# A newly drawn issue order for an attention stage, with eight of its steps on other engines

## The chip, the cores and the metric

One core of one Trainium2 chip runs one program: a gated linear attention followed by two mixture-of-experts layers. The metric is device microseconds of one execution.

## The reference, cut to what matters

```
mag = sqrt(a_re^2 + a_im^2);  scale = min(mag, 0.999) / (mag + 1e-6);  a = (a_re + i*a_im) * scale
for t in range(768):                       # for each of 4 batches x 8 heads, head size 48
    S = a[t][:, None] * S  +  k[t][:, None] * v[t][None, :]      # complex state 48 x 48
    y[t] = q[t] @ real(S)
x = y as 3072 tokens x 384
x = moe(x)        # top-1 of 8 experts, 384 -> 1024 -> 384, relu
out = moe2(x)     # the same form, with a bias by modality in the gate
```

## The kernel before, in words

The recurrence is computed in chunks of 128 tokens. Within a chunk the product of the decays is an exponential of a running sum of logarithms, so a chunk becomes a few matmuls. There are 24 chunks (4 batches x 6); two neighbours of one batch form a unit, so there are 12 units, n = 0 to 11, three to a batch. A unit's elementwise tiles are 128 x 768 (two chunks of 128 x 384, which is 8 heads x 48).

A unit is a list of named steps, each a Python function that issues one to sixteen instructions:

- `ldar ldai ldq ldk ldv` load the five inputs (SyncE's DMA queue).
- `ck` clamps a_re, `sq1` squares it (`x1`), `sq3` squares a_im (`x3`), `ad` adds the two; `ln2 ex2` and `tt` make a_im/a_re, `at` its arctangent; `ln1 ex3 su` make the logarithm of the clamped magnitude.
- `lh ll` split that logarithm into an upper fp16 cast and the rest; `th tl` do the same with the angle. `pL pT` (one per chunk, hence `pL0 pL1`) take the running sums of both with triangular matmuls. `R Ri` are the exponentials of plus and minus the sum, `fi f` take whole turns off the angle, `ab sn cs` make sine and cosine. `cf` and `re` hand the angle and the decay of the unit's last token to the next unit.
- `qR kR` scale q and k. Eight products per unit, `hq/hk` with `c` or `s` (times cosine or sine) and the chunk number, fill the buffers `qhb` and `khb`: `hqs0` is q times sine of chunk 0, `hkc1` is k times cosine of chunk 1.
- For each half chunk (0 to 3): `Tq Tk` transpose on TensorE, `eq ek` copy the result out of PSUM to `qT kT`, `sc` makes the scores, `A` masks them out of PSUM, `py` applies them to v and to the state, `pu` makes the state's update. Per chunk: `S` adds the update to the state, `xe` copies y out of PSUM, `pt` turns it back (and makes the gate's logits), `ye` copies that to `yt`, `lg` sums the logits, `st_` stores. `Sr` decays the state between two units of one batch.

Every engine works its queue off in the order in which the steps are issued. That order isn't worked out in the kernel: each step of unit n has a number in the table `AT` (units 0, 1, 10 and 11 have tables of their own in `AT_OF`), all steps are sorted by n plus that number, and issued in this order. So one step's place in the order says behind which others it stands on its engine. Steps whose names begin with `z` belong to the setting up and to the first expert layer's early work; they keep their numbers. `ENG` says on which engine a step runs that has a choice: A is ScalarE, V is VectorE, P is GpSimd; a copy that isn't in it runs on ScalarE, a product on VectorE. Each step's PSUM bank exists once (`pq pk sc py pu pt pL pT`), so a bank's next matmul waits for the copy that empties it.

The two expert layers behind attention are limited by TensorE and aren't touched.

Of the kernel before, what the change touches and what calls it, by code (L numbers as in the profile page):

```python
# [19 lines left out]
P = 128  # L20
# [19 lines left out]
    zq3=-275.454, ldarb=-273.404, zq2=-255.701, ckb=-206.468, ldara=-199.491, sq1b=-184.693, ln2b=-177.867, zq4=-176.094, cka=-173.23, ldaia=-168.532,  # L40
    sq1a=-158.557, ex2b=-157.908, ln2a=-148.937, sq3a=-139.255, ldaib=-128.596, ldka=-126.962, ada=-126.443, ex2a=-123.863, zq0=-121.356,
    tta=-120.389, ttb=-118.361, zi=-114.402, ln1a=-111.569, zq1=-108.288, sq3b=-107.648, ex3a=-104.749, adb=-93.3771, ata=-91.9742,
    sua=-87.6725, lha=-86.8068, tha=-85.6312, atb=-85.4597, ln1b=-75.4824, tla=-71.2593, ldkb=-69.7035, zw0=-67.7862, ldqa=-67.0486, ex3b=-62.1188,
    thb=-60.4308, lla=-60.1911, zw1=-59.0382, sub=-58.6209, tlb=-57.2903, aba=-54.563, zk0=-53.3853, ldva=-52.7552, sna=-51.9432,
    zw2=-50.8688, lhb=-50.689, qRa=-50.6436, csa=-50.0341, kRa=-49.9225, llb=-49.2676, zw3=-47.5465, ldqb=-42.6622, kRb=-42.4287, zld=-36.0444,
    abb=-34.9246, qRb=-34.251, zw4=-33.8895, csb=-32.1312, snb=-29.7056, zk1=-28.5196, ldvb=-24.0754, zk3=-22.0775, zk2=-20.375, zwh7=-20.0527,
    zwh5=-7.0878, zwh6=-6.1043, ldar=-4.0093, ldai=-3.5899, zf=-3.5878, ck=-3.439, sq3=-3.3275, sq1=-3.1932, ln2=-2.968, ad=-2.8853, ln1=-2.4349,
# [4 lines left out]
    sc0=-0.218, Tq1=-0.2076, ek1=-0.1952, eq1=-0.1787, Tk2=-0.1725, A0=-0.1374, pu0=-0.1229, pu1=-0.0981, Tq2=-0.0816, sc1=0.0506, eq2=0.0589,
    py0=0.0692, A1=0.0795, ek2=0.0816, Tk3=0.0837, Tq3=0.1064, sc2=0.1498, zj=0.1705, A2=0.2304, eq3=0.2386, py1=0.2428, ek3=0.2676, sc3=0.3192,
    S0=0.3254, A3=0.3419, xe0=0.375, pu2=0.4948, py2=0.5072, py3=0.5155, pu3=0.5857, S1=0.7469, pt0=0.8006, Sr=0.9845, xe1=0.999, ye0=1.0899,
    lg0=1.1043, pt1=1.1767, lg1=1.5816, ye1=1.6167, dn0=1.7428, st_0=1.8915, st_1=2.2262, zwl6=2.6952, dn1=2.9886, zwh0=9.4349, zx=18.5444,
# [4 lines left out]
    zl1=146.621, zv3=157.976, zn1=162.009, zn2=187.836, zb1=246.1, zn3=246.175, zy=248.185, zp0=248.274, zp1=248.392, zp2=248.534, zp3=248.627, zp4=248.734,)  # L60
# [3 lines left out]
        pT0=-67.7841, fi0=-67.0196, f0=-61.7138, pL0=-59.0403, R0=-54.7304, Ri0=-52.6787, pT1=-50.8709, fi1=-48.9452, hqs0=-48.6126, pL1=-47.5486,  # L64
        hkc0=-46.3151, Ri1=-45.7758, f1=-44.5775, hqc0=-44.189, cf=-43.3068, hks0=-42.0072, R1=-41.8275, Tq0=-40.999, Tk0=-40.2118, eq0=-39.78,
        ek0=-34.7779, re=-33.8915, Tq1=-33.8833, pu0=-33.0424, eq1=-31.7944, Tk1=-31.2138, sc0=-28.9019, ek1=-27.7924, hks1=-27.3977, hkc1=-24.9845,
        Tk2=-24.9783, A0=-24.6705, ek2=-22.8791, hqs1=-22.187, pu1=-19.2097, sc1=-18.5548, py0=-18.3192, hqc1=-18.0548, A1=-16.0692, Tq2=-15.5424,
# [3 lines left out]
    1: dict(
        ldar=-101.743, ldai=-94.0919, zf=-94.0899, ck=-78.2841, sq1=-71.2758, ln2=-62.5919, sq3=-59.3006, ad=-55.8564, ex2=-50.3502, ln1=-47.8006,
        tt=-44.28, ex3=-43.3419, ldq=-42.2159, at=-41.03, su=-38.5258, lh=-38.2614, th=-34.9928, tl=-34.2366, pT0=-32.1126, ll=-29.8523,
        fi0=-28.1663, pL0=-27.2324, f0=-25.7634, R0=-25.1539, Ri0=-24.9597, pT1=-24.4494, fi1=-24.249, f1=-23.437, pL1=-22.5754, Ri1=-19.7717,
        cf=-18.9824, ab=-17.8481, R1=-17.1808, qR=-16.1147, sn=-15.53, cs=-14.5795, hqs0=-14.4411, ldk=-13.3378, kR=-12.6105, hkc0=-12.47,
        hqc0=-11.9556, hks0=-10.6271, hkc1=-6.2696, Tq0=-6.0733, eq0=-5.8998, Tk0=-5.7469, hks1=-4.2407, ek0=-4.1023, Tk1=-3.5527, sc0=-2.6519,
        hqs1=-1.9267, ek1=-1.7986, Tk2=-1.6539, Tq1=-1.3874, A0=-1.3585, ldv=-1.2862, re=-1.0837, eq1=-1.063, sc1=-1.0134, ek2=-0.939, A1=-0.9329,
        py0=-0.8977, Tk3=-0.844, hqc1=-0.7965, py1=-0.7448, ek3=-0.6767, pu0=-0.6229, Tq2=-0.5093, xe0=-0.4163, eq2=-0.3254, sc2=-0.2386, Tq3=-0.1498,
        eq3=0.0114, A2=0.0134, S0=0.1126, pt0=0.1643, sc3=0.1952, A3=0.2118, pu2=0.2324, py2=0.2469, py3=0.3399,),
    10: dict(  # L80
        Ri0=-1.4969, ab=-0.9638, Tk0=-0.032, ek0=0.249, eq0=0.5548, Tk1=0.7965, pu0=1.3833, Tq1=1.7056, eq1=1.7221, sc0=1.8233, A0=1.9039, Tq2=2.5052,
        pu1=4.282, ek1=4.3357, sc1=6.6333, eq2=8.0424, A1=8.8523, Tk2=10.8171, ek2=11.3936, py0=11.5196, py1=11.8605, xe0=12.7758, Tq3=13.1808,
        sc2=14.2779, Tk3=14.4721, eq3=14.5258, ek3=15.125, pt0=15.8254, ye0=16.5362, S0=16.5795, A2=17.3647, sc3=18.7283, pu2=20.2593, pu3=21.189,
        A3=21.687, lg0=24.0486, st_0=24.3998, py2=24.78, py3=25.3316, S1=28.3151, Sr=28.7014, xe1=30.6519, pt1=32.5238, ye1=35.8667, st_1=37.718,
        lg1=39.4762,),
    11: dict(
        sq3=-3.125, fi0=-1.5816, Ri0=-1.4225, pT1=-0.97, fi1=-0.5837, f1=-0.4329, pL1=-0.3027, ab=0.5919, R1=0.6353, qR=5.7779, Ri1=6.187, sn=6.5754,
        kR=7.5733, cs=8.0961, hkc0=9.6684, hqs0=12.8295, hqs1=14.9143, hqc0=15.2924, Tq0=15.4494, hks0=15.656, Tk0=15.9411, ek0=16.0465, eq0=16.6374,
        hqc1=16.9535, Tk1=22.094, ek1=22.8709, hkc1=23.1684, hks1=23.2614, Tq1=23.4143, sc0=24.344, A0=25.4597, Tk2=26.6705, eq1=29.7717, sc1=31.0878,
        Tq2=31.3853, A1=31.9494, ek2=32.1395, Tk3=32.4928, ek3=32.5899, pu0=32.7076, py0=33.0527, eq2=33.1787, py1=36.0196, sc2=36.4618, A2=39.3626,  # L90
        Tq3=39.4329, pu1=40.0651, xe0=41.1663, S0=41.3977, pt0=44.0857, eq3=44.9432, sc3=45.3048, A3=45.5878, ye0=45.8481, py2=45.8729, py3=46.7035,
        lg0=49.6787, xe1=52.1539, st_0=55.6457, pt1=58.3812, lg1=61.6312, ye1=62.8647, dn0=66.0238, st_1=67.1457, dn1=72.3027, dn2=79.4783,),
# [1232 lines left out]
```

## Time and profile before

| | |
|---|---|
| time, median of 3 runs | 803.96 us (799.52 to 807.28) |
| the profiled execution | 801.56 us, of which its span 799.8 us |
| attention's steps, by the trace | 0 to about 283 us of the span |
| the rest | the two expert layers |

Read it like this: the profiled execution's time is its span plus 1.8 us around it, and all rows below are of that execution. A stretch is given in microseconds from the span's start. "Busy" is the time in which an engine's instructions ran, waits inside an instruction included.

### The profile page before, as it was taken

To read this page: it belongs to the slowest core of one execution; us is meant where nothing else is said; L and a number is where in the kernel's file an instruction comes from. 1 tells how busy PE (TensorE), PEld (TensorE's weight loads), DVE (VectorE), ACT (ScalarE), POOL (GpSimd) and SP (SyncE) were. 2 spreads that over 40 slices of the span, in tenths; PEclk is the share of its full clock that TensorE was granted. 3 is DMA by queue.
4 is the path that set the end of the run, shared out by engine and by line. 5 is a ranking of instruction groups with operands and counts; after the bars stand their busy time and mean duration, and the time that the engine had idled before them with its cause. 6 is when DMAs were issued, how large, how long until landed. Compare 5 with 4: busy or idle time off the path is not lost. (4 is left out here: it accounts for less than half of the span.)

```text
span 799.8 us, 23480 instructions
## 1 busy us (share of the span) xinstructions
PE 736.1 (92%) x8451; PEld 595.8 (74%) x8451; DVE 562.9 (70%) x1437; ACT 469.2 (59%) x1008; POOL 284.2 (36%) x266
## 2 busy tenths in 40 slices
PE   7787889989898998999999999999898999999995
PEld 3475769768786976878787877788676787877873
DVE  8889999999999877575747486864473345545455
ACT  7797788787796525473737465675322345533453
POOL 5556575565676121221221224221121221312211
PEclk9898999998999999999999999999998999999998
DMA  9949674775433151625334252524033111511110
GB/s 185 249 80 197 143 150 120 169 153 122 93 81 100 38 202 34 208 56 185 110 126 161 87 191 76 187 70 169 19 99 133 41 58 46 208 52 42 60 44 29
DMA packets 159262, 91.41 MB, mean 114 GB/s; under 512 B 131804, under 2 KB 149764, under 8 KB 159104
## 3 DMA queue, kind: packets, MB, share of 16 engines
q1 hardware_dynamic: 151872, 68.49, 33.3%
q0 software_dynamic: 7232, 21.05, 8.5%
q8 instruction: 71, 1.16, 0.6%
q14 instruction: 87, 0.71, 0.3%
HBM read 192.54 MB, written 20.84 MB: 267 GB/s over the span
## 5 line engine op out<-in xcount | busy, mean ns | idle before, releaser
L817 PEld LDWEIGHTS <-wh 128*128 128x128 f16 x1296 | 127.9, 99 | 14.3 <-ACTq L882 6.4
L818 PEld LDWEIGHTS <-wh 128*128 128x128 f16 x1296 | 127.7, 99 | 7.9 <-issue 1.0
L819 PEld LDWEIGHTS <-wl 128*128 128x128 f16 x1296 | 127.8, 99 | 0.0
L838 POOL DMA_INDIRECT x<-yo,r1ids x27 | 31.8, 1178 | 182.2 <-ACT yo L837 126.0
L741 DVE SCALAR_TENSOR_TENSOR wl<-ws,wh 128x768 f16<-128x768 f32 x88 | 82.8, 952 | 15.4 <-ACT wh L740 7.5
L740 ACT ACTIVATE wh<-ws 128x768 f16<-128x768 f32 x88 | 74.1, 845 | 10.3 <-ACTq L852 4.8
L830 PE MATMUL mpu<-wh,hl 128*128 128x384 f16 x216 | 70.5, 327 | 5.2 <-DVE hl L822 4.4
L830 PEld LDWEIGHTS <-hl 128*128 128x128 f16 x432 | 42.4, 98 | 43.8 <-DVE hl L822 13.0
L830 PE MATMUL mpy<-wh,hl 128*128 128x384 f16 x216 | 71.1, 329 | 3.1 <-DVE hl L822 1.8
L828 PE MATMUL mpy<-wh,hh 128*128 128x384 f16 x216 | 71.2, 330 | 0.8 <-ACT hh L821 0.8
L817 PE MATMUL msc<-xh,wh 128*128 128x128 f16 x384 | 68.0, 220 | 3.8 <-ACTq L882 3.8
L829 PE MATMUL mpy<-wl,hh 128*128 128x384 f16 x216 | 71.0, 329 | 0.0
L828 PE MATMUL mpu<-wh,hh 128*128 128x384 f16 x216 | 70.4, 326 | 0.0
L829 PE MATMUL mpu<-wl,hh 128*128 128x384 f16 x216 | 70.4, 326 | 0.0
L817 PE MATMUL mpk<-xh,wh 128*128 128x128 f16 x384 | 68.0, 220 | 1.8 <-ACTq L882 1.8
L838 POOL DMA_INDIRECT out_dram<-yo,r2ids x21 | 21.1, 1005 | 134.8 <-ACT yo L837 127.6
L819 PE MATMUL mpq<-xh,wl 128*128 128x128 f16 x384 | 68.4, 220 | 0.0
L817 PE MATMUL mpq<-xh,wh 128*128 128x128 f16 x384 | 68.4, 220 | 0.0
L818 PE MATMUL mpq<-xl,wh 128*128 128x128 f16 x384 | 68.4, 220 | 0.0
L819 PE MATMUL msc<-xh,wl 128*128 128x128 f16 x384 | 68.1, 220 | 0.0
L818 PE MATMUL msc<-xl,wh 128*128 128x128 f16 x384 | 68.1, 220 | 0.0
L819 PE MATMUL mpk<-xh,wl 128*128 128x128 f16 x384 | 68.1, 220 | 0.0
(510 smaller groups left out, 2270.9 us busy)
## 6 DMA issues: line engine op xcount, KB each, us to landing
ws<-in_moe_w_dram SPq DMA_DIRECT2D x100, 1536.0 KB
ar<-in_a_re_dram SPq DMA_DIRECT2D x24, 192.0 KB
ai<-in_a_im_dram SPq DMA_DIRECT2D x24, 192.0 KB
k<-in_k_dram SPq DMA_DIRECT2D x24, 192.0 KB
q<-in_q_dram SPq DMA_DIRECT2D x24, 192.0 KB
v<-in_v_dram SPq DMA_DIRECT2D x24, 192.0 KB
x<-zero SPq DMA_DIRECT2D x8, 576.0 KB
x<-yt SPq DMA_DIRECT2D x24, 192.0 KB
```

The lines of the kernel that those rows point to most:

```text
L740: nc.scalar.activation(H_,S_,AF.Copy,scale=WS,accum_out=s.fl[:,s.n:s.n+1]); s.n+=1
L741: if lo: nc.vector.scalar_tensor_tensor(L_,S_,WS,H_,op0=ALU.mult,op1=ALU.subtract)
L817: nc.tensor.matmul(o,W.h1[:,d,fs],x.h[:,d,:],start=(d==0),stop=False)
L818: nc.tensor.matmul(o,W.h1[:,d,fs],x.l[:,d,:],start=False,stop=False)
L819: nc.tensor.matmul(o,W.l1[:,d,fs],x.h[:,d,:],start=False,stop=(d==ND-1))
L828: nc.tensor.matmul(o,hh[:,r,:],W.h2[:,f,:],start=(f==0),stop=False)
L829: nc.tensor.matmul(o,hh[:,r,:],W.l2[:,f,:],start=False,stop=False)
L830: nc.tensor.matmul(o,hl[:,r,:],W.h2[:,f,:],start=False,stop=(f==NF-1))
L838: nc.gpsimd.indirect_dma_start(out=s.dst,out_offset=bass.IndirectOffsetOnAxis(ap=R.ids[:,j:j+1] if ids is None else ids(),axis=0),in_=y,in ...
```

## The change: what it does

All numbers of `AT` and `AT_OF` for attention's own steps are new; the `z` steps keep theirs. Eight kinds of step change engine in units 1 to 11: `sq1`, `lh` and `eq2` go from VectorE to ScalarE, `ek0`, `ek1` and `ye0` from ScalarE to VectorE, `hqs0` and `hkc1` from VectorE to GpSimd. Unit 0 has the same for its copies and products, but of its half-wide passes only `sq1a` (to ScalarE) and `tta` (from GpSimd to VectorE) move. Two steps get the code for it:

```
 AT=dict(
...
-    ex2=-2.1973, ex3=-2.1849, su=-2.0713, lh=-2.061, tt=-1.9721, at=-1.8171, th=-1.8089, tl=-1.7655, ll=-1.7159, pL0=-1.6663, pT0=-1.6333,
...
+    ex3=-2.5125, ex2=-2.4717, su=-2.4082, tt=-2.3592, lh=-2.0144, at=-1.9704, ll=-1.6353, pL0=-1.6327, th=-1.6191, ldq=-1.6042, tl=-1.5858,
...
 ENG=dict(
-    ek0="A", ek1="A", ek2="A", ek3="A", eq0="A", eq1="A", eq3="A", xe0="A", xe1="A", ye0="A", ye1="A", Sr="P", hkc0="P", hks0="P", hks1="P", hqc1="P",
-    hqs1="P", kR="P", kRa="P", kRb="P", qR="P", sq3="A", tt="P", tta="P", ttb="P", eq2="V", hkc1="V", hqc0="V", hqs0="V",
-    qRa="V", qRb="V", sq1="V", sq1a="V", sq1b="V", sq3a="V", sq3b="V", th="V", tha="V", thb="V",)
+    ek2="A", ek3="A", eq0="A", eq1="A", eq2="A", eq3="A", lh="A", sq1="A", sq1a="A", sq3="A", xe0="A", xe1="A", ye1="A", Sr="P", hkc0="P", hkc1="P",
+    hks0="P", hks1="P", hqc1="P", hqs0="P", hqs1="P", kR="P", kRa="P", kRb="P", qR="P", tt="P", ttb="P", ek0="V", ek1="V", hqc0="V", lha="V", lhb="V",
+    qRa="V", qRb="V", sq1b="V", sq3a="V", sq3b="V", th="V", tha="V", thb="V", tta="V", ye0="V",)
...
-        def sq1(nm,s,sl): eng(nm).tensor_mul(s(tile_("x1")),s(u.x2),s(u.x2))
+        def sq1(nm,s,sl):
+            if ENG[nm]=="A": nc.scalar.activation(s(tile_("x1")),s(u.x2),AF.Square)
+            else: eng(nm).tensor_mul(s(tile_("x1")),s(u.x2),s(u.x2))
...
-        def lh(nm,s,sl): V.tensor_scalar(out=s(tile_("lh",F16)),in0=s(u.x1),scalar1=CS,scalar2=None,op0=ALU.mult)
+        def lh(nm,s,sl):
+            t=s(tile_("lh",F16))
+            if ENG.get(nm,"V")=="A": nc.scalar.activation(t,s(u.x1),AF.Copy,scale=CS)
+            else: V.tensor_scalar(out=t,in0=s(u.x1),scalar1=CS,scalar2=None,op0=ALU.mult)
```

Sorted by these numbers, one unit's worth of the middle of the stage reads as follows (n is the unit whose scores are made; a plus counts units ahead, a minus units behind; GpSimd's list begins where its queue turns to the scaling of q):

```
before
VectorE  A0(n) f1(+1) su lh(+2) eq2(n) A1(n) lg0(-1) ad(+3) cf(+1) th(+2) A2(n) tl ll(+2) re(+1) S0(n) A3(n) hqs0 hqc0(+1) ck(+4) lg1(-1) fi0 f0(+2) hkc1(+1) S1(n) sq1(+4) fi1(+2)
ScalarE  ln2(+3) ek2(n) ye0(-1) at(+2) eq3(n) ab(+1) ek3(n) sn(+1) xe0(n) cs(+1) Ri0 R0(+2) ln1(+3) ye1(-1) sq3(+4) ek0 eq0(+1) ex2(+3) ek1(+1) ex3(+3) eq1(+1) Ri1 R1(+2) xe1(n)
GpSimd   qR kR hks0 hkc0 hqs1 hks1 hqc1(+1) Sr(n) tt(+3)
after
VectorE  A0(n) re(+1) lg1(-1) cf(+1) A1(n) ll th(+2) ad(+3) S0(n) tl(+2) A2(n) ye0 lg0(n) fi0(+2) hqc0(+1) A3(n) f0(+2) ek0(+1) ck(+4) su(+3) fi1(+2) S1(n) f1(+2) ek1(+1)
ScalarE  at(+2) eq2(n) sq3(+3) ab(+1) ek2(n) sn(+1) ye1(-1) xe0 eq3(n) cs(+1) ek3(n) R0 Ri0(+2) ln1 ln2 ex3(+3) eq0(+1) ex2(+3) R1(+2) xe1(n) Ri1(+2) eq1(+1) sq1(+4) lh(+3)
GpSimd   qR kR hks0 hqs0 hkc0 hks1 hqs1 hkc1 hqc1(+1) tt(+3) Sr(n)
```

On the load queue, at the start, the first half of unit 0's v and unit 1's q, which stood ahead of the first expert's weights (two loads of 1,536 KB), stand behind them, and unit 1's a_re stands ahead of the second half of unit 0's a_im. Later on, the load queue keeps the same loads and stores in another order; the loads that matter for a unit still stand half a unit and more ahead of its first use. On TensorE, unit 1's `pT0 pL0 pL1 pT1` stand ahead of unit 0's `Tq1`, where they stood behind its `Tk1`.

## Rows read from the trace of the kernel before

**Rows 1.** The page: span in 40 equal slices, busy tenths; PEclk is the granted clock.
```profile
PE   7787889989898998999999999999898999999995
...
DVE  8889999999999877575747486864473345545455
...
PEclk9898999998999999999999999999998999999998
```

**Rows 2.** Busy time by stretch, three units each: PE, PEld, DVE, ACT, POOL, granted clock, DMA.
```profile
60.50:121.60 61.10, 49.94 (x522) 40.51 (x523) 60.38 (x82) 46.95 (x72) 37.84 (x25) 0.87 0.76 158
121.60:183.00 61.40, 56.52 (x643) 48.28 (x641) 58.86 (x96) 49.75 (x78) 38.32 (x26) 0.92 0.68 146
```

**Rows 3.** Groups of VectorE, 121.6 to 183.0: count, busy us, mean ns, idle before.
```profile
L213 DVE TENSOR_SCALAR lh<-x 128x768 f16<-128x768 f32 x3 | 6.3, 2096 | 0.1
L224 DVE SCALAR_TENSOR_TENSOR tl<-x,th 128x768 f16<-128x768 f32 x3 | 4.5, 1498 | 0.0
L274 DVE TENSOR_TENSOR qhb<-q,fi 128x384 f32<-128x384 f32 x3 | 4.0, 1349 | 0.0
...
L211 DVE SCALAR_TENSOR_TENSOR x<-x,x 128x768 f32<-128x768 f32 x3 | 3.7, 1231 | 0.0
L215 DVE SCALAR_TENSOR_TENSOR ll<-x,lh 128x768 f16<-128x768 f32 x3 | 3.6, 1210 | 0.0
...
L197 DVE TENSOR_TENSOR x<-x 128x768 f32<-128x768 f32 x3 | 2.8, 950 | 0.0
L274 DVE TENSOR_TENSOR qhb<-q,f 128x384 f32<-128x384 f32 x3 | 2.8, 917 | 0.0
...
L168 DVE COPY qT<-pq 112x512 f32<-112x512 f32 x3 | 2.0, 678 | 0.0
...
L274 DVE TENSOR_TENSOR khb<-k,fi 128x384 f32<-128x384 f32 x3 | 1.6, 549 | 0.0
...
L315 DVE COPY st<-pu 112x384 f32<-112x384 f32 x1 | 0.6, 558 | 0.0
```

**Rows 4.** Timeline of GpSimd and VectorE at 26.6, 129 and 138: start, length.
```profile
26.65 0.56 DVE L213 TENSOR_SCALAR lh<-x 128x768 f16<-128x768 f32 x1
...
129.29 1.83 POOL L259 TENSOR_TENSOR q<-q,Rb 128x768 f32<-128x768 f32 x1 [0.97 <-ACT Rb L156]
129.44 2.10 DVE L213 TENSOR_SCALAR lh<-x 128x768 f16<-128x768 f32 x1
...
137.81 1.00 POOL L274 TENSOR_TENSOR khb<-k,fi 128x384 f32<-128x384 f32 x1
```

**Rows 5.** Groups of GpSimd, 121.6 to 183.0.
```profile
L274 POOL TENSOR_TENSOR qhb<-q,f 128x384 f32<-128x384 f32 x3 | 4.3, 1444 | 0.0
L274 POOL TENSOR_TENSOR khb<-k,fi 128x384 f32<-128x384 f32 x3 | 3.4, 1138 | 2.6 <-ACT fi L156 2.5
...
L341 POOL TENSOR_TENSOR st<-st,re 112x384 f32<-112x384 f32 x2 | 3.0, 1475 | 5.9 <-DVE st L316 5.9
```

**Rows 6.** Groups of ScalarE, 121.6 to 183.0.
```profile
L167 ACT COPY kT<-pk 112x512 f32<-112x512 f32 x12 | 7.2, 596 | 1.7 <-PE pk L284 1.5
...
L167 ACT COPY yt<-pt 128x384 f32<-128x384 f32 x6 | 3.1, 514 | 4.0 <-DVE r1lg L1085 4.0
...
L194 ACT ACTIVATE x<-ai 128x768 f32<-128x768 f32 x3 | 2.5, 846 | 0.0
```

**Rows 7.** Waits, 121.6 to 183.0: who waited for whom, total, times, longest.
```profile
POOL khb L274 <- issue: 10.4, 3, 4.6
...
PE pL L227 <- DVE ll L215: 2.0, 1, 2.0
...
DVE A L292 <- PE psc L289: 1.4, 2, 0.8
```

**Rows 8.** Timeline of the load queue and TensorE at the start.
```profile
15.26 1.69 SPq L733 DMA_DIRECT2D ws<-in_moe_w_dram  x2
...
30.90 0.31 PE L308 MATMUL pu<-v,khb 128*48 128x48 f32 x1
```

More of the change, by code (lines that the diff above doesn't have):

```diff
@@ L39 @@
 AT=dict(
[L40 to L47, printed above, removed]
@@ L48 @@
-    ex2=-2.1973, ex3=-2.1849, su=-2.0713, lh=-2.061, tt=-1.9721, at=-1.8171, th=-1.8089, tl=-1.7655, ll=-1.7159, pL0=-1.6663, pT0=-1.6333,
-    Ri0=-1.561, R0=-1.4721, fi0=-1.3936, f0=-1.3709, pL1=-1.3399, ldq=-1.3337, pT1=-1.2634, fi1=-1.1436, f1=-1.1064, ldk=-1.1002, Ri1=-1.0362,
-    R1=-1.0279, qR=-0.9287, cf=-0.8378, ab=-0.7366, sn=-0.72, re=-0.7118, kR=-0.6994, hqs0=-0.6457, cs=-0.5981, hks0=-0.4886, hkc0=-0.4783,
-    hqc0=-0.4618, ldv=-0.406, Tq0=-0.3957, hqs1=-0.3915, Tk0=-0.3812, hks1=-0.3461, hqc1=-0.3357, hkc1=-0.3233, ek0=-0.3089, Tk1=-0.2469, eq0=-0.2262,
@@ L52 @@
[L52 to L55, printed above, removed]
@@ L56 @@
-    dn2=19.4824, zwh2=22.9948, zwh4=25.1415, zec0=27.4267, zwh1=27.8833, zec1=31.1581, zec2=32.499, zes0=36.406, zes1=39.3171, zes2=40.4556,
-    zb0=40.2, zwl0=40.4969, zg0=43.5134, zwl2=44.0341, zwl5=46.1229, zg1=46.5527, zwh3=47.1601, zs0=48.8419, zwl7=49.0052, zt0=50.3089, zwl4=50.9329,
+    zq3=-275.454, ldarb=-264.9366, zq2=-255.701, ckb=-255.2219, ldara=-254.8635, sq1b=-254.7775, cka=-246.2329, ln2b=-245.3372, sq1a=-186.1661,
+    ex2b=-185.5438, ldaia=-178.5193, ln2a=-176.1276, sq3a=-176.1186, ada=-176.1098, ex2a=-176.1039, zq4=-176.094, tta=-142.1405, zq0=-121.356,
@@ new lines @@
+    ldaib=-121.2119, ln1a=-119.4429, zi=-114.402, sq3b=-114.0996, ata=-113.924, ldka=-113.3893, adb=-113.2573, tha=-113.0078, ex3a=-112.8417,
+    zq1=-108.288, sua=-108.2532, ldqa=-108.1621, ln1b=-102.7579, lha=-95.5511, zw0=-67.7862, lla=-67.5617, ttb=-67.543, tla=-67.5336, ex3b=-60.9673,
+    sub=-59.2026, lhb=-59.0997, zw1=-59.0382, zk0=-53.3853, ldqb=-53.3816, kRa=-53.3802, atb=-50.9528, thb=-50.9075, tlb=-50.8802, llb=-50.8716,
+    zw2=-50.8688, aba=-48.2571, zw3=-47.5465, ldkb=-45.6871, csa=-45.6746, sna=-45.6585, qRa=-45.6266, abb=-41.2423, zld=-36.0444, csb=-35.4916,
@@ new lines @@
+    zw4=-33.8895, snb=-33.8869, ldva=-32.3857, qRb=-28.9291, zk1=-28.5196, zk3=-22.0775, kRb=-20.8793, zk2=-20.375, zwh7=-20.0527, ldvb=-7.6984,
+    zwh5=-7.0878, zwh6=-6.1043, ldar=-4.03, zf=-3.5878, ldai=-3.4105, ck=-3.4097, sq1=-3.0855, sq3=-2.9701, ad=-2.6001, ln1=-2.5145, ln2=-2.5138,
+    ex3=-2.5125, ex2=-2.4717, su=-2.4082, tt=-2.3592, lh=-2.0144, at=-1.9704, ll=-1.6353, pL0=-1.6327, th=-1.6191, ldq=-1.6042, tl=-1.5858,
+    pT0=-1.5524, R0=-1.547, fi0=-1.5398, Ri0=-1.5358, ldv=-1.5354, f0=-1.5216, pL1=-1.5124, pT1=-1.5111, R1=-1.4687, ldk=-1.4045, Ri1=-1.4044,
@@ new lines @@
+    fi1=-1.4016, f1=-1.3988, re=-1.1695, cf=-0.9722, qR=-0.971, ab=-0.9699, sn=-0.6365, kR=-0.6337, hks0=-0.6029, hqs0=-0.585, cs=-0.5549,
+    hkc0=-0.5545, hks1=-0.547, hqs1=-0.5433, Tk0=-0.5359, hqc0=-0.5358, Tq0=-0.535, eq0=-0.5124, hkc1=-0.5034, ek0=-0.4694, Tq1=-0.4692, Tk1=-0.4092,
+    sc0=-0.4087, hqc1=-0.4036, eq1=-0.4019, ek1=-0.357, A0=-0.3524, Tq2=-0.105, pu0=-0.0199, sc1=-0.0183, pu1=0.0293, Tk2=0.0293, eq2=0.0298,
+    py0=0.03, A1=0.0301, zj=0.1705, ek2=0.3622, Tq3=0.3643, py1=0.3651, S0=0.4002, Tk3=0.4007, xe0=0.4077, sc2=0.4092, eq3=0.4092, pu2=0.4188,
@@ new lines @@
+    A2=0.4237, ek3=0.4453, pt0=0.4456, pu3=0.4519, ye0=0.4527, sc3=0.4528, lg0=0.4598, py2=0.4639, A3=0.4672, py3=0.4998, xe1=0.5527, S1=0.6012,
+    pt1=0.6448, lg1=1.0276, Sr=1.029, st_0=1.0298, ye1=1.4024, dn0=1.5026, st_1=1.9808, dn1=2.6018, zwl6=2.6952, zwh0=9.4349, zx=18.5444, dn2=19.7371,
+    zwh2=22.9948, zwh4=25.1415, zec0=27.4267, zwh1=27.8833, zec1=31.1581, zec2=32.499, zes0=36.406, zes1=39.3171, zb0=40.2, zes2=40.4556,
+    zwl0=40.4969, zg0=43.5134, zwl2=44.0341, zwl5=46.1229, zg1=46.5527, zwh3=47.1601, zs0=48.8419, zwl7=49.0052, zt0=50.3089, zwl4=50.9329,
@@ L58 @@
     ze=51.2097, zT0=56.3585, zc0=56.6477, zs1=61.8791, zl0=62.3709, zm0=63.218, zt1=63.7944, zwl1=65.9349, zh0=67.4886, zv0=71.8316, zm1=78.3957,
     zm2=80.9205, zh1=81.4287, zwl3=83.2655, zm3=86.1353, zv1=86.7572, zT1=98.9824, zn0=109.241, zc1=114.441, zh2=116.542, zh3=125.501, zv2=131.272,
-    zl1=146.621, zv3=157.976, zn1=162.009, zn2=187.836, zb1=246.1, zn3=246.175, zy=248.185, zp0=248.274, zp1=248.392, zp2=248.534, zp3=248.627, zp4=248.734,)
+    zl1=146.621, zv3=157.976, zn1=162.009, zn2=187.836, zb1=246.1, zn3=246.175, zy=248.185, zp0=248.274, zp1=248.392, zp2=248.534, zp3=248.627,
@@ L62 @@
+    zp4=248.734,)
 AT_OF={
     0: dict(
[L64 to L67, printed above, removed]
@@ L68 @@
-        eq2=-15.3171, Tk3=-14.5155, py1=-14.2345, xe0=-13.5341, Tq3=-13.1601, S0=-12.8812, eq3=-10.7242, sc2=-10.2014, pt0=-8.6395, A2=-8.4514,
-        ek3=-8.1457, ye0=-6.687, sc3=-5.5362, py2=-4.0031, A3=-3.8729, py3=-3.1622, pu2=-1.6498, pu3=-1.5134, lg0=-0.9969, xe1=-0.311, S1=-0.2738,
-        Sr=-0.156, pt1=-0.0217, lg1=0.2903, ye1=0.9742, st_0=1.6002,),
-    1: dict(
[L72 to L79, printed above, removed]
@@ L80 @@
-    10: dict(
[L81 to L85, printed above, removed]
@@ L86 @@
-    11: dict(
[L87 to L92, printed above, removed]
+        pL0=-67.5529, pT0=-59.1084, fi0=-59.0936, Ri0=-59.0689, R0=-52.3876, f0=-51.8196, pT1=-47.991, fi1=-45.7227, pL1=-45.6929, R1=-45.6308,
@@ new lines @@
+        Ri1=-45.6154, f1=-45.1871, cf=-40.829, re=-37.0406, hqs0=-35.525, hkc0=-35.5003, hks0=-35.2185, hqc0=-33.8862, Tk0=-33.3212, Tq0=-33.321,
+        hqs1=-28.8059, eq0=-20.0658, ek0=-19.7488, hqc1=-13.3169, Tq1=-7.6642, pu0=-7.358, pu1=-7.3535, eq1=-6.3712, Tk1=-3.3378, hks1=-3.3077,
+        hkc1=-2.9415, S0=-2.7488, ek1=-1.9123, sc0=-1.5685, A0=-1.5614, Tq2=-1.2232, pu2=-1.2102, Tk2=-1.1192, eq2=-1.1182, pu3=-1.115, py0=-1.1141,
+        ek2=-1.1137, sc1=-1.1023, A1=-1.0178, Tk3=-0.9703, Tq3=-0.566, ek3=-0.5563, eq3=-0.5149, sc2=-0.5143, A2=-0.5059, py1=-0.4989, xe0=-0.4897,
@@ new lines @@
+        sc3=-0.4333, pt0=-0.2777, A3=-0.1413, ye0=0.057, py2=0.1636, py3=0.198, lg0=0.3641, xe1=0.3867, S1=0.4533, Sr=0.4645, pt1=0.5068, lg1=0.5952,
+        ye1=1.3291, st_0=1.3673,),
+    1: dict(
+        ldar=-122.2447, ck=-118.7214, ldai=-111.041, sq1=-68.5471, ln2=-60.0846, ex2=-56.9239, sq3=-53.2917, ad=-52.0168, tt=-51.9253, at=-47.9791,
+        th=-46.6208, ln1=-42.588, ex3=-37.3201, su=-36.2627, lh=-36.1864, tl=-34.871, ll=-34.321, pT0=-34.3209, fi0=-34.3127, pL0=-29.9243,
+        f0=-29.9203, R0=-29.5866, Ri0=-22.4378, pL1=-19.6401, R1=-18.0473, Ri1=-16.2534, pT1=-8.6717, fi1=-8.4218, f1=-8.219, ldk=-7.2703,
+        ldq=-4.4455, ab=-2.7035, cf=-2.5673, kR=-2.5652, cs=-2.5614, qR=-2.4893, hkc0=-2.2758, sn=-2.225, re=-2.1309, hqs1=-2.0421, hks0=-1.9986,
+        hqs0=-1.9704, Tk0=-1.5026, hkc1=-1.5001, ldv=-1.449, ek0=-1.4431, hqc0=-1.4378, Tq0=-1.4305, Tk1=-1.4192, hqc1=-1.4097, hks1=-1.4083,
+        eq0=-1.3907, Tq1=-0.8344, ek1=-0.8342, eq1=-0.8097, Tk2=-0.6367, sc0=-0.5888, Tq2=-0.5863, pu0=-0.5203, A0=-0.5192, py0=-0.4913, eq2=-0.4082,
+        ek2=-0.4032, Tq3=0.0297, sc1=0.0338, Tk3=0.0387, A1=0.0388, py1=0.3043, xe0=0.4126, eq3=0.4157, S0=0.4162, sc2=0.4256, pt0=0.4496, A2=0.4516,
+        pu2=0.4518, ek3=0.4519, sc3=0.457, py2=0.4689, A3=0.4875, py3=0.5219,),
@@ new lines @@
+    10: dict(
+        Ri0=-1.5539, ab=-0.9712, eq0=-0.4979, Tk0=-0.4053, ek0=-0.1036, Tk1=0.0277, sc0=0.7494, Tq1=0.7519, pu0=0.7567, ek1=1.4627, A0=1.6015,
+        eq1=1.8231, Tk2=1.8243, sc1=1.8248, Tq2=1.9627, py0=4.4609, A1=6.4672, eq2=6.7564, ek2=6.9082, py1=7.0288, Tq3=8.272, sc2=11.6037,
+        pu1=11.7032, xe0=11.7276, Tk3=12.5124, eq3=13.1036, ek3=13.1527, S0=13.3673, A2=13.4097, pt0=15.0475, ye0=15.1973, sc3=15.2236, A3=15.2358,
+        py2=17.428, pu2=17.4299, lg0=17.4308, py3=18.0597, pu3=26.4085, xe1=26.4185, S1=26.4723, pt1=26.4802, ye1=26.4873, lg1=26.5282, st_0=30.2202,
+        Sr=31.9702, st_1=53.6001,),
@@ new lines @@
+    11: dict(
+        sq3=-3.3998, fi0=-1.536, Ri0=-1.4981, pT1=-1.4279, fi1=-1.2243, pL1=-1.0127, f1=-0.9962, R1=-0.2456, Ri1=0.4687, ab=0.5224, qR=0.5385,
+        kR=0.8233, sn=0.8234, cs=1.9193, hqs0=10.7193, hqc0=12.1152, hkc0=12.3445, Tq0=12.503, hks0=12.504, hkc1=13.7743, eq0=13.9012, Tq1=14.1402,
+        hqs1=14.177, Tk0=16.9149, ek0=16.9526, eq1=17.0015, hqc1=17.0187, Tq2=25.408, Tk1=25.4086, eq2=25.4698, Tq3=25.5518, sc0=25.5652, pu0=29.219,
+        ek1=29.2192, hks1=29.2197, A0=29.22, Tk2=29.2205, ek2=30.1283, sc1=30.4591, Tk3=31.0328, A1=31.0793, py0=33.9283, sc2=35.3688, pu1=35.4882,
+        A2=36.5036, ek3=36.6086, eq3=37.448, py1=37.6666, sc3=38.0008, S0=39.3703, A3=39.3853, xe0=41.3988, pt0=43.479, py2=48.1531, py3=50.2777,
+        xe1=51.5924, ye0=51.792, lg0=52.4969, pt1=52.5183, lg1=55.2838, dn0=62.7472, ye1=68.3041, st_0=72.5776, st_1=72.6059, dn1=72.7172, dn2=78.7804,),
```

## The prediction

> **What bounds the kernel now.** The page's 40 slices come first [rows 1]: VectorE stands at 8 and 9 tenths through the first 13 slices, which are attention, and falls afterwards, where TensorE is at 9. So the change touches a stage of some 283 of 800 us that VectorE limits. The stretches say how firmly: three units take 61.4 us, 20.5 us each, and VectorE is busy in 58.86 of it (19.6 a unit); TensorE 56.52 at a granted clock of 0.92 (18.8 a unit, waits and slow stretches included), ScalarE 49.75 (16.6), GpSimd 38.32 (12.8) [rows 2]. In the list of waits VectorE hardly appears (1.4 us on scores), while others wait for it, as TensorE does for `ll` [rows 7]. VectorE is the bound, but TensorE is 4% behind it.
>
> Next: what is VectorE's time made of? Its groups [rows 3] show passes of one shape at different lengths. The product `hkc1` takes 0.549 us, `hqs0` 0.917, `hqc0` 1.349, all 128 x 384. The cast `lh` takes 2.096, and the timeline shows why: at 26.65 it needs 0.56; at 129.44 it starts while GpSimd's scaling of q runs (129.29, 1.83 long) and ends 0.42 us after it [rows 4]. So a VectorE pass with two SBUF inputs, or this fast cast, stands still until GpSimd's running instruction is through. By the same comparison (a full-width pass alone is 0.95, as `sq1`) `tl` loses 0.55 us, `su` 0.28, `ll` 0.26, `hqc0` 0.80, `hqs0` 0.37, `lh` 1.54: 3.8 us a unit of waiting inside instructions. Passes out of PSUM don't lose any: `eq2` has a mean of 0.678, the state's copy 0.558 [rows 3]. In reverse GpSimd's products, 1.00 alone [rows 4], have means of 1.138 and 1.444, and `Sr` 1.475 [rows 5].
>
> **Part by part, per unit.** *VectorE loses* `lh` (2.096), `hqs0` (0.917), `hkc1` (0.549), `sq1` (0.950), `eq2` (0.678): 5.19 us. *It gains* `ek0` and `ek1`, of `eq2`'s shape, 2 x 0.678, and `ye0`, priced by the state's copy of 384 columns out of PSUM, 0.56: 1.92 [rows 3]. Net 3.27 as measured; without the waits inside `lh` and `hqs0` (1.91) the work alone falls by 1.36. Whether the waits go with the instructions is the main question. Lower end: they all come back at the next pass that needs GpSimd's silence, and VectorE comes to 19.6 - 1.4 = 18.2 us. Upper end: none comes back, 16.3. The passes that remain (`su ll tl ad th hqc0`) now wait 1.9 us of the 3.8; GpSimd will be running 75 to 80% of the time instead of 62, so I take them a quarter up (0.5), and 16.8 to 18.2 for VectorE.
>
> *GpSimd gains* `hqs0` and `hkc1`: 1.444 + 1.138 = 2.6 us as measured, 2.0 alone [rows 4, 5]; 12.8 becomes 15.4.
>
> *ScalarE* gains `sq1` and `lh`, each priced by the square of a_im at 0.846, and `eq2` at 0.596, and gives up `ek0`, `ek1` (2 x 0.596) and `ye0` (0.514) [rows 6]: +0.6, 17.2. An `lh` that writes fp16 isn't in the trace on ScalarE; between 0.5 and 1.1 it moves the sum by 0.3 either way. The table switches stay the same in number: arctangent, sine and cosine are still one group and exp and log the other.
>
> *What excludes what.* The full waits inside instructions mean that GpSimd's time and that of VectorE's two-input passes can't overlap. Per unit, GpSimd alone: `tt qR kR` 3 x 1.83, five products at 1.00, `Sr` at 1.0 (an estimate by the product's row) in two units of three: 11.2. VectorE's share: `su ll tl ad` 4 x 0.95, `sq1` 0.95, `lh th` 2 x 0.56, three products 3 x 0.55: 7.5. Sum 18.7 of 20.5. After: GpSimd 13.2; VectorE 4 x 0.95 + 0.56 + 0.55 = 4.9; sum 18.1. That is a second limit, and the change moves it by only 0.6 us: it takes 0.56 + 0.95 off VectorE, but two products of 0.55 become two of 1.00. The Trainium skill says this as a rule (SBUF — State Buffer, "Who interferes with whom"): GpSimd and a VectorE instruction with two SBUF inputs or in a two-port mode take turns under an exclusive lock, and the later one blocks fully. The trace agrees, with 2.10 us for a cast of 0.56. The rule speaks against moving products to GpSimd.
>
> *The order.* `Sr` now stands behind `tt`, so 1.8 us later on GpSimd, and TensorE's next `py0` needs it; against that GpSimd no longer stands idle for `S`, 5.9 us in three units [rows 5]. `py0` has `Tq2 pu0 sc1 Tk2 pu1` ahead of it as cover. `hks0` stands idle 10.4 us in three units for something that the profile doesn't name [rows 7]; it still comes right behind `kR`, so this gap may stay, now with `hqs0` behind it too. `eq3` and `cs` stand behind `xe0` on ScalarE, which waits for `py1`: if `Sr` is late, GpSimd's next cosine products are late too. I cost the order at 0 in the middle, between -0.5 and +1.0 us a unit; nothing in the trace settles it.
>
> *Start and end.* Unit 0's first half of v now comes behind the weights. Their loads are issued at 15.26 and the first `pu` runs at 30.90 [rows 8], so 15.6 us cover 3.1 MB, which at the 158 GB/s of the next stretch [rows 2] would take 19.9: a risk of up to 4 us, though a load with nothing beside it should do better. Unit 1's sums ahead of `Tq1` delay unit 0 by some microseconds and bring unit 1 forward. I take 0 for both, -2 to +5 together. The last unit keeps its form.
>
> **The sum.** After the change four limits lie close: VectorE 16.8 to 18.2, GpSimd and VectorE by turns 18.1, TensorE 18.8 at the clock of 0.92 and 17.3 if all of it ran at full clock, ScalarE 17.2. Now the period is 0.9 us above the highest (20.5 against 19.6). With the highest at 18.5 and 0.9 on top a unit takes 19.4, 1.1 less. That counts for the nine units of the two stretches' kind and about half of the work at either end: 10 units, 11 us. The profiled execution's 801.56 becomes 790.6; it lies 2.4 under the median, so I forecast **792 us** for a median. The rest of the kernel is limited by TensorE and only starts earlier.
>
> **The rivals.** *The turn-taking decides* (2 in 10). If what held VectorE was really its turns with GpSimd, the period follows the second limit: 18.7 to 18.1, 0.6 us, 10 units, 6 us: 798 by the median. For it: 3.8 us of such waits a unit. Against it: the sum reaches 91% of the period, VectorE's own 96%. By the Trainium skill's rule on the lock it would be this one.
>
> *More than that* (1.5 in 10). TensorE's clock rises as its waits go (the granted clock is 0.87 and 0.92 here and 1.0 in most later slices [rows 1, 2]), the passes that remain meet GpSimd rarely, and a unit takes 18.2: 2.3 x 10 = 23 us, 781.
>
> *GpSimd becomes the bound, and it is slower* (1.5 in 10). GpSimd is idle 23.1 us in three units now, 7.7 a unit, mostly for its inputs [rows 2]. With 15.4 us of work it may wait 5.1 at today's period; above that the period grows. If the sines, cosines and states come no sooner than now and only part of the idle time is filled, so that 6.2 remain, a unit takes 21.6: 1.1 x 10 = 11 us slower, 815. For it: ScalarE, which makes those inputs, gets 0.6 us more work, and `Sr` stands behind `tt`. Against: the long waits were for VectorE's late `S` and for ScalarE in VectorE's step.
>
> **How the numbers follow.** The forecast has 5 in 10, with a range of its own of 785 to 798 (VectorE's two ends and the order's cost). The range over all goes from 778 to 809: below lies the better part of "more than that", above the worse half of GpSimd's case. A change of about 1%, 8 us, is what can be told from none: faster means under 796. That holds for seven eighths of the forecast's 0.5, all of "more than that" and a fifth of the turn-taking: 0.44 + 0.15 + 0.04 = 0.63. Slower than 812 holds for two thirds of GpSimd's case and a little of the start's risk: 0.13. Within: 0.24.
>
> **What would show it.** In the changed profile's stretches of three units: VectorE busy clearly less than now and with idle time of its own in the list of waits; the period near 19.4; GpSimd near 15.4 a unit. `tl`, `ll`, `su` and `hqc0` show by their means whether the waits of `lh` came back (all back: 1.9 us more over them). `ek0`, `ek1` at 0.68 and `ye0` at 0.56 must not be stretched. If GpSimd's idle time is above 5 us a unit or the first `pu` comes after 35 us, the forecast is wrong on the slow side; a granted clock near 1.0 with periods under 18.5 would make it wrong on the fast one.

## The result, and the profile after

After takes 783.49 us (median of 4, 779.86 to 784.17) against 804.38 of before in the same comparison: ratio 0.9737 [0.968, 0.9794]. On a second chip, in later runs, it was 0.969 [0.9647, 0.9733]. The forecast was 792 us; the attention part of the profiled execution came out 11.3 us shorter, as forecast, and about 6 us came from a place that the forecast left out.

The page of after, the slices that answer to [rows 1]:

```profile
PE   7688999899899989999999999999899999999994
...
DVE  7888898899789978474747586764564435445354
...
PEclk9799999899899999999999999999999999999997
```

VectorE stands more often at 7 and 8 in the first 13 slices. The stretches of three units that answer to [rows 2], busy us of TensorE, its loads, VectorE, ScalarE, GpSimd, then the granted clock:

```profile
81.60:141.30 59.70, 54.99 (x656) 45.94 (x656) 54.53 (x91) 54.38 (x82) 47.52 (x34) 0.98 0.80 165
141.30:202.10 60.80, 55.85 (x640) 46.59 (x641) 52.84 (x91) 52.26 (x79) 42.41 (x32) 0.95 0.62 125
```

VectorE has fallen from 60.4 and 58.9 us to 54.5 and 52.8, GpSimd and ScalarE have risen, and no engine fills the stretch any more. VectorE's groups from 141.3 to 202.1, which answer to [rows 3]:

```profile
L169 DVE COPY kT<-pk 112x512 f32<-112x512 f32 x7 | 4.8, 685 | 1.1 <-PE pk L290 1.1
...
L221 DVE SCALAR_TENSOR_TENSOR ll<-x,lh 128x768 f16<-128x768 f32 x3 | 3.7, 1219 | 0.0
L230 DVE SCALAR_TENSOR_TENSOR tl<-x,th 128x768 f16<-128x768 f32 x3 | 3.6, 1205 | 0.0
...
L214 DVE SCALAR_TENSOR_TENSOR x<-x,x 128x768 f32<-128x768 f32 x3 | 2.9, 953 | 0.0
...
L280 DVE TENSOR_TENSOR qhb<-q,fi 128x384 f32<-128x384 f32 x3 | 2.7, 894 | 0.0
...
L463 DVE TENSOR_TENSOR r1oh<-im,rtmi 128x48 bf16<-128x48 f32 x1 | 1.9, 1853 | 0.0
L261 DVE CAST cfb<-f 32x384 f16<-32x384 f32 x2 | 1.8, 911 | 0.0
L169 DVE COPY yt<-pt 128x384 f32<-128x384 f32 x3 | 1.7, 558 | 0.4 <-PE pt L326 0.4
```

`ll` is as before, `tl`, `su` (L214) and `hqc0` (L280) are 0.3, 0.3 and 0.5 us shorter: in these four the waits of `lh` didn't come back. They came back in others. The routing at a batch's end (`r1oh`, and `r1acc`, which stands in the last section) and the cast in `cf` are longer than in before's stretch of [rows 3], whose rows for them are

```profile
L468 DVE TENSOR_TENSOR r1acc<-r1acc,rtsu 128x8 bf16<-128x8 bf16 x1 | 1.4, 1442 | 0.1
...
L255 DVE CAST cfb<-f 32x384 f16<-32x384 f32 x2 | 0.7, 356 | 0.0
...
L457 DVE TENSOR_TENSOR r1oh<-im,rtmi 128x48 bf16<-128x48 f32 x1 | 0.2, 207 | 0.0
```

These three groups take 2.3 us in before and 7.3 in after, 1.7 us a unit more. So VectorE's time fell by 2.0 us a unit, between the 1.4 that the prediction gave for all waits coming back and the 3.3 for none. The two moved steps on ScalarE, and the longest waits of GpSimd and VectorE, in the same stretch:

```profile
L199 ACT ACTIVATE x<-x 128x768 f32<-128x768 f32 x3 | 2.6, 855 | 1.0 <-DVE x L192 1.0
...
L218 ACT ACTIVATE lh<-x 128x768 f16<-128x768 f32 x3 | 2.5, 849 | 0.0
```

```profile
POOL khb L280 <- ACT f L157: 8.1, 2, 7.1
DVE A L298 <- PE psc L295: 3.6, 5, 1.8
```

The table divides each profiled span at three instructions: unit 2's first `A`, unit 9's first `A`, the last copy to `yt`. *Jump* is TensorE's wait at the branch into the second expert layer (the first layer's is in the last section). The experiments ran four to a chip, on three chips (before's medians there: 817.14, 815.54, 805.58 us); ratios are against before on the same chip, the parts are one execution each.

| kernel | ratio, 95% interval | start | middle | end | rest | jump |
|---|---|---|---|---|---|---|
| before, first profile | | 83.3 | 144.0 | 55.9 | 516.7 | 3.80 |
| after, first profile | 0.9737 [0.968, 0.9794] | 81.6 | 139.0 | 51.3 | 510.4 | 1.34 |
| order_only (chip 1) | 1.005 [1.0017, 1.0082] | 86.5 | 150.8 | 54.4 | 525.6 | 1.33 |
| engines_only | 0.9998 [0.9967, 1.0028] | 86.6 | 143.6 | 59.4 | 527.2 | 1.33 |
| products_back | 0.9697 [0.9636, 0.9758] | 82.1 | 140.0 | 53.5 | 517.8 | 1.33 |
| lh_back | 0.9886 [0.982, 0.9953] | 83.6 | 147.1 | 51.5 | 522.4 | 4.37 |
| before_again (chip 2) | | 85.5 | 148.7 | 56.0 | 526.8 | 5.04 |
| after_again | 0.969 [0.9647, 0.9733] | 80.0 | 138.3 | 51.2 | 518.1 | 1.33 |
| engines_lh_later | 0.9917 [0.9886, 0.9948] | 85.7 | 138.3 | 60.5 | 523.6 | 1.33 |
| after_lh_close | 0.968 [0.9635, 0.9724] | 80.4 | 139.5 | 51.3 | 515.1 | 1.33 |
| new_ends (chip 3) | 1.0109 [1.0086, 1.0131] | 93.3 | 145.8 | 62.1 | 515.7 | 1.34 |
| lh_only_later | 0.9871 [0.985, 0.9891] | 84.3 | 138.9 | 56.1 | 514.8 | 3.83 |
| sq1_back | 0.9947 [0.9923, 0.997] | 82.7 | 150.3 | 51.2 | 513.9 | 3.38 |
| krb_first | 0.9744 [0.9719, 0.9768] | 81.1 | 138.6 | 51.2 | 510.9 | 1.34 |

Before's middle differs by 4.7 us between its two profiles, after's by 0.7; before_again's execution took 818.77 us, 3.2 above the median there. So the change gains 1.7 to 5.5 us at the start, 5.0 to 10.4 in the middle, 4.6 to 4.8 at the end, and 6.3 to 8.7 behind attention.

The middle is two batches (six units) and one step from unit to unit more, and these steps aren't alike. Over two whole batches, from unit 2's first `A` to unit 8's or from unit 3's to unit 9's, before takes 122.9 or 122.2 us, after 120.5 or 121.7; before_again takes 127.3 or 126.9, after_again 119.6 or 121.0. So a unit gained 0.1 to 0.4 us on the first pair of profiles and 1.0 to 1.3 on the second. On the first pair most of the middle's 5.0 us lies in the step across a batch's end (from unit 2 to unit 3, 21.8 us in before and 17.3 in after).

### The profile page after: what moved, and what is told of

It is laid out like the page before. It is cut to its first block, busy times and chain, and to the rows that moved or that the text cites. A ratio compares the mean times of both kernels' runs of the same rounds, so it can differ in the third digit from the quotient of the medians.

```text
span 782.3 us, 23431 instructions
## 1 busy us (share of the span) xinstructions
PE 730.2 (93%) x8451; PEld 587.4 (75%) x8451; DVE 533.9 (68%) x1415; ACT 474.5 (61%) x1007; POOL 297.9 (38%) x289
## 5 line engine op out<-in xcount | busy, mean ns | idle before, releaser
L747 DVE SCALAR_TENSOR_TENSOR wl<-ws,wh 128x768 f16<-128x768 f32 x88 | 83.6, 962 | 13.1 <-ACTq L858 7.2
L824 PE MATMUL mpk<-xl,wh 128*128 128x128 f16 x384 | 68.4, 220 | 0.0
```

The lines of the kernel that those rows point to most:

```text
L747: if lo: nc.vector.scalar_tensor_tensor(L_,S_,WS,H_,op0=ALU.mult,op1=ALU.subtract)
L824: nc.tensor.matmul(o,W.h1[:,d,fs],x.l[:,d,:],start=False,stop=False)
```

## The experiments

**The two halves of the change, and parts of it undone** (the code is after's in all four).

```diff
 order_only:    AT, AT_OF of after;  ENG of before
 engines_only:  AT, AT_OF of before; ENG of after
 products_back: after with
-    hqs0="P", hkc1="P"
+    hqs0="V", hkc1="V"
 lh_back: after with
-    lh="A"
+    lh="V"
```

> The new order with the engines of the kernel before. If the engine moves make the gain (theory M), VectorE keeps its 19.6 us a unit and the time stays with the kernel before, 799 to 808. If the order makes it (theory O), 783 to 792. If order and engines only work together, slower than before, over 810.

> The old order with the engines of the changed kernel. M: most of the gain, 785 to 794. O: little of it, 799 to 806. If they only work together: over 806.

> The changed kernel with two products (hqs0, hkc1) back on VectorE from GpSimd. M: VectorE's 17.6 us a unit become 18.6 to 19.4 and the period grows by 0.2 to 0.8: 786 to 792. If taking turns with GpSimd is the limit (theory L), GpSimd's 2.0 us a unit turn into VectorE's 1.1, the period falls by up to 0.9: 774 to 782.

> The changed kernel with lh (the upper cast of the decay) back on VectorE from ScalarE. M: VectorE gets 0.56 us a unit plus up to 1.5 of waiting for GpSimd: 784 to 793. If ScalarE is the limit of the changed kernel (17.4 us a unit), 0.85 less there makes it faster: 775 to 781.

In the whole time neither half gains anything alone: the order costs 0.5%, the engine moves measure as nothing. By parts it is less clear, since before wasn't profiled on this chip. Against before_again, whose chip has the nearest median, engines_only is 5.1 us shorter in the middle and 4.5 longer at the two ends; against the first before its middle is 0.4 shorter.

The two products are worth nothing on either engine (0.9697 against 0.969 and 0.9737 of after), which misses theory M's 786 to 792 too (0.977 to 0.985 of before). With them back GpSimd has less to do and VectorE more, and the middle isn't shorter (140.0 against 139.0 and 138.3), though theory L forecast up to 0.9 us a unit: the sum of their turns isn't a limit. `lh` put back on VectorE in its new slot makes the middle some 7 us longer (147.1 against 140.0 of products_back on the same chip), so ScalarE wasn't the limit either.

One wait that stands against the engine moves in the old order shows in engines_only's list of waits from 129.6 to 190.9 (us in total, times, longest), and in its timeline (start, length):

```profile
129.60:190.90 61.30, 53.05 (x637) 45.32 (x637) 52.78 (x90) 50.69 (x79) 43.16 (x33) 0.97 0.73 146
```

```profile
POOL q L264 <- ACT Rb L156: 7.9, 3, 2.8
ACT lh L217 <- DVE x L213: 6.0, 3, 2.5
```

```profile
148.77 1.81 POOL L207 TENSOR_TENSOR x<-ai,x 128x768 f32<-128x768 f32 x1
149.28 2.12 DVE L213 SCALAR_TENSOR_TENSOR x<-x,x 128x768 f32<-128x768 f32 x1
...
151.43 0.84 ACT L217 ACTIVATE lh<-x 128x768 f16<-128x768 f32 x1 [2.30 <-DVE x L213]
152.18 0.47 ACT L156 ACTIVATE Ri<-pL 128x384 f32<-128x384 f32 x1
152.55 0.48 ACT L156 ACTIVATE Rb<-pL 128x384 f32<-128x384 f32 x1
...
153.11 1.82 POOL L264 TENSOR_TENSOR q<-q,Rb 128x768 f32<-128x768 f32 x1 [2.53 <-ACT Rb L156]
```

VectorE is busy in 52.8 of 61.3 us, as in after, and the unit takes 20.4 us (20.5 in [rows 2], 20.9 in the same units of before_again). `lh` stands right behind `su` in the old order. On one engine neither waits for the other; now ScalarE stands idle for 2.30 us while `su`, itself held by GpSimd's `tt`, is made, and behind `lh` wait `Ri`, `R` and GpSimd's scaling of q.

**One place in the order.**

```diff
 engines_lh_later: engines_only with
-    lh=-2.061
+    lh=-1.93
 after_lh_close: after with
-    lh=-2.0144
+    lh=-2.4081
```

> Before's order with after's engines, and one number of that order changed: lh from -2.061 to -1.93, so that ScalarE reaches the cast behind Ri0 R0 xe1 of other units and not right behind su. In engines_only ScalarE stands idle 6.0 us in three units for su at this cast, and behind it wait Ri0 R0, GpSimd's scaling of q (7.9 us in three units) and TensorE's py. Theory room (an engine move pays only where the step stands late enough behind the one that feeds it on another engine): the wait at lh falls under 1.5 us in three units, a unit gets 0.5 to 1.5 us shorter, 5 to 15 us: ratio 0.982 to 0.994 against 0.9998 of engines_only. Rival whole (no single place matters, the gain is in the new order as a whole): the wait shows up elsewhere, ratio 0.996 to 1.004.

> After, with one number of its order changed: lh from -2.0144 to -2.4081, right behind su (-2.4082). Theory room: ScalarE now waits at lh for su, about 2 us a unit, and loses 0.5 to 1.5 us a unit: ratio 0.979 to 0.992 against 0.974 of after. Rival whole: it stays within 0.3% of after.

> Before itself, for a profile on the chip of the other runs. Theory chip (the 6 us that after gained behind attention, in the expert layers, are a difference between executions): attention ends here 10 to 13 us later than in after on this chip, and the expert layers behind it take the same within 3 us. Rival carried on (the change shortens the expert layers as well): they take 5 us or more longer than after's on this chip.

> After itself, on the chip of the other runs. Ratio 0.968 to 0.979 again. Theory chip: 10 to 13 us are gained up to attention's last copy to yt and what is left lies in the expert layers and changes sign or size from run to run. Rival carried on: the same 5 us or more once more in the expert layers.

The one number brings the middle of engines_only from 143.6 to 138.3 us, which is after's, and the ratio from 0.9998 to 0.9917, as theory room had it. Over two whole batches it brings 0.4 to 2.3 us; the rest lies again in the step across a batch's end (22.0 us from unit 2 to unit 3 in engines_only, 17.1 here). In engines_lh_later the three units from 125.1 take 58.80 us, and the wait at `lh` is 2.9 us (theory room had it under 1.5); over all units it falls from 16.6 us in ten waits to 6.3 in two:

```profile
125.10:183.90 58.80, 53.45 (x645) 46.59 (x645) 51.82 (x90) 51.89 (x79) 42.78 (x33) 0.97 0.76 152
```

```profile
ACT lh L217 <- DVE x L213: 2.9, 1, 2.9
```

Something else changes with the number. The cast in `cf`, which the next unit's cosine and sine need, no longer meets GpSimd; engines_only's row, then engines_lh_later's:

```profile
L260 DVE CAST cfb<-f 32x384 f16<-32x384 f32 x2 | 3.7, 1865 | 0.0
```

```profile
L260 DVE CAST cfb<-f 32x384 f16<-32x384 f32 x2 | 0.7, 356 | 0.0
```

So that the place of `lh` makes the gain is shown; that it does so by the wait on ScalarE alone isn't.

The counter-test didn't produce its wait: with `lh` right behind `su`, after_lh_close has 3.7 us of idle time at `lh` over all units, not 2 a unit, and stays at after's time, as rival whole had it. In the new order `su` is made early enough. So the number's distance by itself decides nothing; that the wait does is theory room's reading, which this run couldn't test. The repeated profiles speak against theory chip, which put the 6 us behind attention down to the execution: on one chip the rest takes 526.8 us in before and 518.1 in after (last section). Attention ends 20.7 us later in before_again, not 10 to 13.

**What is enough, and what the new order needs.**

```diff
 lh_only_later: before with lh on ScalarE (after's code for lh), and
-    lh=-2.061
+    lh=-1.93
 sq1_back: after with
-    sq1="A"
+    sq1="V"
 new_ends: engines_lh_later, but units 0, 1, 10, 11 with after's numbers
 krb_first: after with
-    kRb=-20.8793
+    kRb=-28.81
```

> Before with one engine move, lh to ScalarE, and its number at -1.93; all other steps keep engine and number. Theory lh (the cast is what VectorE and GpSimd keep each other waiting with; the other seven moves are worth little): from unit 2 to unit 9 it takes 138 to 142 us (before 148.7), VectorE's waits inside instructions fall from 5.2 us a unit to 3.5 or less, ratio 0.985 to 0.992. Rival all moves (VectorE is still full without them): the waits come back in su, tl, ll and the products, 145 us or more, ratio above 0.994.

> After with the square sq1 back on VectorE, 0.95 us a unit there instead of 0.85 on ScalarE. Theory VectorE counts: a unit is 0.3 to 0.9 us longer, attention 3 to 9 us. Rival: nothing, as with the two products. Apart from that, on the wait of ScalarE at its jump into the second expert layer (3.3 and 4.5 us in both profiles of before and 3.9 in lh_back, none in the others, with a granted clock of 0.5 to 0.9 for some 16 us behind it): this kernel has as many ScalarE instructions ahead of that jump as lh_back, 11 fewer than after. If the wait hangs on the place of the jump in ScalarE's code, it is here again, 3 to 5 us, with the low clock behind it; if it hangs on when the transfers run, it need not be. With it the ratio is 0.978 to 0.988, without 0.969 to 0.978.

> After's engines; units 2 to 9 in before's order with lh at -1.93 (as in engines_lh_later), units 0, 1, 10 and 11 in after's order. Read from the profiles so far, on these chips: from unit 2's first scores to unit 9's before takes 148.7 us, engines_only 143.6, engines_lh_later 138.3, after 138.3; from the start to unit 2 they take 85.5, 86.6, 85.7 and 80.0, from unit 9 to the last copy to yt 56.0, 59.4, 60.5 and 51.2. Theory places (in the middle the new order is worth no more than lh's place, and the rest of its gain is in the first two and last two units): attention ends within 2 us of after's 269.5, ratio 0.966 to 0.977 (a jump of ScalarE that waits at the first expert layer may cost 3 us of it). Rival whole (the orders of the ends and the middle only work together): attention ends 5 us or more later, ratio 0.980 or above.

> After with one number changed: unit 0's second half of k is scaled (kRb) ahead of hqs1 and not behind it on GpSimd. In after, ScalarE's Ri of unit 1 waits 1.81 us for kRb, TensorE's pL1 of unit 1 3.21 us for that Ri, and unit 0's Tq1 stands behind it. Theory start: the first pu comes 2 to 3 us sooner than at 37.0, and the whole of it is left at the end: ratio 0.2 to 0.4% under after's 0.969. Rival: unit 2's scores come no sooner, since something else in units 0 and 1 ends last; no difference from after.

`lh` alone, with its place, takes the middle to 138.9 us, and two whole batches to 120.4 or 120.6, as theory lh had it. The other seven moves and the whole new order add nothing there that shows (138.3 to 139.0). In the new order, though, one square put back on VectorE costs all of it: 150.3, which is beyond the 3 to 9 us and the ratio of 0.978 to 0.988 that were forecast. Two neighbouring units of sq1_back show how (GpSimd, then VectorE; L265 is `kR`, L198 `sq1`, L340 `re`, L259 and L260 `cf`):

```profile
169.24 1.83 POOL L265 TENSOR_TENSOR k<-k,Ri 128x768 f32<-128x768 f32 x1
```

```profile
150.12 0.32 DVE L340 COPY re<-pr 64x8 f32<-64x8 f32 x2
150.46 0.96 DVE L198 TENSOR_TENSOR x<-x 128x768 f32<-128x768 f32 x1
...
169.24 0.33 DVE L340 COPY re<-pr 64x8 f32<-64x8 f32 x2 [0.57 <-PE pr L337]
169.59 2.29 DVE L198 TENSOR_TENSOR x<-x 128x768 f32<-128x768 f32 x1
171.81 0.18 DVE L1089 TENSOR_REDUCE r1lg<-pt 128x8 f32<-128x32 f32 x1
172.01 0.36 DVE L259 CAST cfb<-f 32x384 f16<-32x384 f32 x1
172.41 0.55 DVE L260 TENSOR_TENSOR cfb<-f,cfb 32x384 f16<-32x384 f32 x1
```

With GpSimd idle the square takes 0.96 us, beside `kR` 2.29, until `kR` is through; and `cf` stands behind it. The square's mean over 126.1 to 191.3 is 2319 ns, and ScalarE and GpSimd wait longer for what follows than in after's stretch, where the same two waits come to 3.0 and 2.2 us:

```profile
126.10:191.30 65.20, 57.81 (x647) 47.85 (x643) 58.13 (x93) 49.61 (x76) 43.25 (x33) 0.92 0.67 137
```

```profile
ACT qT L166 <- PE pq L285: 8.8, 3, 4.1
POOL x L206 <- ACT x L155: 6.6, 3, 3.8
```

In lh_only_later, where the old order gives the same square another slot, its mean is 950 ns; `su` (L211) waits there instead, 2.71 us against 1.23 in [rows 3], and the middle is short all the same:

```profile
L211 DVE SCALAR_TENSOR_TENSOR x<-x,x 128x768 f32<-128x768 f32 x3 | 8.1, 2707 | 0.0
...
L197 DVE TENSOR_TENSOR x<-x 128x768 f32<-128x768 f32 x3 | 2.9, 950 | 0.0
```

order_only has the square at 2630 ns and a middle of 150.8 us; that this slot is what the order alone loses by fits, but wasn't tested by itself. Theory places is half right: the middle needs only `lh`, but these two orders couldn't be joined, and attention ends at 301.2 us, not at 269.5. In new_ends it takes 29.4 us from unit 8's first `A` to unit 9's and 29.5 on to unit 10's, at the seam, and unit 2 begins at 93.3; what each end's order is worth couldn't be separated in this way. krb_first brings the first `pu` to 34.87 us, and unit 2 comes at 81.1, no sooner than in after (81.6 and 80.0); its time is after's. No kernel tried beats after by more than the noise.

## Why the prediction was right, point by point

**The bound.** VectorE was busy in 96% of a unit, as the prediction said. That less work for it shortens a unit by as much was not so: engines_only takes 6 us off three units of VectorE (58.86 in [rows 2], 52.78 here) and leaves the unit at 20.4 us, 0.1 to 0.5 shorter.

**The failed step: "I cost the order at 0 in the middle".** The sum credited the engine moves with the whole 11 us; alone they are worth 0.9998. In its place the runs show that single slots of the order decide: with `lh` one number later the same moves measure 0.9917, and in the new order one square in a slot beside `kR` makes the middle 11.7 us longer (150.3 against 138.6 of krb_first on the same chip). The reading that fits these runs is that a moved step needs room behind the step that feeds it, and the passes left on VectorE mustn't meet a long GpSimd instruction at a place on which the unit waits. The wait that took the place of the one removed was in sight: `su` and `lh` are neighbours in the list of VectorE's steps, and the prediction moved the second to another engine without asking what that engine would do meanwhile.

**The terms.** VectorE at 18.2 and 17.6 us a unit: forecast 16.8 to 18.2. GpSimd 15.8 and 14.1: forecast 15.4. ScalarE 18.1 and 17.4: forecast 17.2, with `lh` at 0.85 inside its 0.5 to 1.1. The copies on VectorE, at 0.685 and 0.558, weren't stretched. The waits of `lh` left the four passes that the prediction watched, but 1.7 us a unit came back in `cf` and the routing, which its list of passes doesn't have; so VectorE came out in the upper half of its range. The period, forecast 1.1 us shorter, fell by 0.1 to 0.4 on the first chip and by 1.0 to 1.3 on the second, over whole batches. Start and end, whose order was costed at 0, gave 1.7 and 4.6 us, and the step across a batch's end most of the middle's 5.0. So 11.3 us in attention is the forecast's 11 by errors that cancel: the number was luck.

**"The rest only starts earlier"** was wrong by 6.3 and 8.7 us.

**The rivals.** Turn-taking as a sum fell with products_back. As single waits it counts, and here the Trainium skill's rule on the lock (SBUF — State Buffer, "Who interferes with whom") is borne out: 0.96 against 2.29 us for one square. GpSimd as the bound didn't come: it waits for ScalarE (8.1 us in three units), and no unit grew. More than that, 781, lay nearest the measured 783.49, but not for its reasons: the clock in attention rose to 0.98 and 0.95, but the periods, 19.9 and 20.3 us, stayed above 18.5.

**The signs.** Two were badly chosen: GpSimd idle 6.1 us a unit in the second stretch and a first `pu` at 37.0 us were to mean a slow result. Both came, and the result was fast. krb_first has the first `pu` 2.1 us sooner and gains nothing by it; GpSimd's idle time was tested by no run. What sets the 19.9 to 20.3 us of a unit now, with TensorE at 18.3 to 18.6, stays open.
